# Moving the second layer's weight conversion and the experts' result stores in a retention + MoE + SoLU kernel

## Chip, core and metric

One core of a Trainium2 chip runs the whole kernel. The metric is the device time of one execution in microseconds (us). Time before: median 525.42 us of three runs (524.66 to 526.79).

Engines are named as in the profile: PE (TensorE, matmuls), PEld (its weight loads), DVE (VectorE), ACT (ScalarE), POOL (GpSimd), and SP, which here only issues DMAs. Each engine works through its instructions in program order, and an instruction that waits holds up everything behind it on its engine. "SPq" in a row is a DMA that SP issues.

## What is computed

Three stages follow each other: a retention over 768 steps (chunked into tiles), a top-2-of-8 mixture of experts, and a two-layer block with a SoLU between its layers.

```python
def _moe_ref(x, w_gate, w_noise, noise, w1, w2):      # x: 1536 x 512, 8 experts
    ...
    for e in range(E):
        for k in range(2):
            mask = top2[:, k] == e
            h = np.maximum(x[mask] @ w1[e], 0.0)       # 512 -> 1024
            out[mask] += top2_w[mask, k, None] * (h @ w2[e])   # 1024 -> 512

def _moe2_ref(x, w_in, w_out, g_ln):
    h = x @ w_in                                       # 512 -> 1024
    ...                                                # softmax of h, h * softmax, layer norm, g_ln
    return (ln @ w_out).astype(np.float32)             # 1024 -> 512
```

[...]

## The kernel before

**Matmuls in three terms.** Every fp32 operand is split into a high part (rounded to fp32r, by ACT) and a low part (the rest, by DVE): `xh`/`xl` for rows, `wh`/`wl` for weights, `hh`/`hl` for hidden values. A product is three matmuls: high x high, high x low, low x high.

**Experts.** A loop (lines 1051 to 1105) runs experts e = 0 to 6, sorted by load, with 448 down to 388 rows; the last one, e = 7 with 384 rows, has a code of its own (lines 1110 to 1154). The first layer (`hidden`) makes eight blocks f = 0..7 of 128 hidden columns: 12 matmuls into one PSUM bank, then ACT writes `hh` (line 707) and DVE writes `hl` (line 708). The banks alternate between the tags `b` and `a`, two of each, so block f can start only when `hl` of block f-4 is done. The second layer of e = 0..6 (`second`, line 1039) accumulates transposed results in the four banks c0..c3; during the first layer of the expert after it, `y_t` (line 1022) transposes each bank on DVE into `yr`, and after the fourth four DMAs on SP (line 1026) store it to `yg` in DRAM. The second layer of e = 7 (line 1146) makes rows at once: three row blocks b = 0, 1, 2, evicted by ACT (`y_rows`, line 1127) and stored to `yg`.

**Weights.** Weights arrive in units of 512 KB, eight for each expert and eight (64 to 71) for `w_in` (64 to 67) and `w_out` (68 to 71). `load_unit` issues the DMA on SP into one of four raw buffers `wr`; `split_unit` makes `wh` on ACT (line 194, for `w_out` line 190) and `wl` on DVE (line 195, for `w_out` line 191). `feed(split_to, load_to)` does both up to given units, and `advance(e, j)` calls it after each quarter of a layer.

**Conversion.** `convert_steps` is a generator of 16 jobs, eight for each of the two matrices, and `convert()` takes it one step further. A job has two steps: A (lines 117 to 119 on DVE, then line 120 on ACT) and B (lines 123 and 124 on DVE, which need ACT's result, then a DMA store on SP, line 125, and the load of a later job's raw bits, line 102). A first call only loads. So the generator is through after 33 calls. Before, e = 0 makes 6 calls and each of e = 1..6 makes 5 (two within the first layer, one after each of the last three quarters of the second); line 1108 would run the rest, and nothing is left by then.

**The way into the last block.** `weights` (line 668, called in the last expert after block 5) computes on DVE where each token's two results lie in `yg`. After block b = 0 of the last expert is stored, POOL gathers the results of the first tokens (line 799), ACT and DVE mix them (lines 809 and 810), and PE transposes the mixed rows (`x2_t`, line 819). That first transpose stands six hidden blocks into row block b = 2.

Of the kernel before, what the change touches and what calls it, by code (L numbers as in the profile page):

```python
# [44 lines left out]
def retnet_moe_solu(ctx, tc, qT, kT, k, v, w_gate, w_noise, noise, w1, w2, w_in, w_out, g_ln,  # L45
                    decay, out, dbg=None):
    nc = tc.nc
    B, NC, _, H, D = v.shape
# [3 lines left out]
    E = w1.shape[0]  # L52
# [28 lines left out]
    conv_jobs = []  # L81
    conv_ctx = ExitStack()
    def to_f32(w, name):
        if w.dtype == F32:
            return w
        rows, cols = w.shape
        f = dram.tile([rows, cols], F32, name=name)
        n = rows * cols // 128
        for c in range(0, n, 512):
            conv_jobs.append((w, f, c))  # L90
        return f

    def convert_steps():
        V = nc.vector
        cv = conv_ctx.enter_context(tc.tile_pool(name="cv", bufs=1, side="right", reuse_waits="tile"))
        view = lambda x, c: x.rearrange("(p r) f -> p (r f)", p=128)[:, c:c + 512]

        def load(n):
            if n < len(conv_jobs):
                w, _, c = conv_jobs[n]  # L100
                t = cv.tile([128, 512], I64, tag="raw", name="raw", bufs=2)
                nc.sync.dma_start(t, view(w, c))
                raws.append(t)

        raws = []
        load(0)
        for n, (w, f, c) in enumerate(conv_jobs):
            load(n + 1)
            yield
            raw = raws.pop(0)  # L110
            bits = raw.bitcast(I32).rearrange("p (n t) -> p n t", t=2)
            l, h = raw.bitcast(U32).rearrange("p (n t) -> p n t", t=2)[:, :, 0], bits[:, :, 1]
            m, e = (cv.tile([128, 512], I32, tag=t, name=t) for t in ("cm", "ce"))
            t = m.bitcast(F32)
            o = cv.tile([128, 512], F32, tag="co", name="co", bufs=2)

            V.tensor_scalar(m, h, 0xFFFFF, 1 << 20, op0=OP.bitwise_and, op1=OP.bitwise_or)
            V.scalar_tensor_tensor(t, l, 2.0 ** -32, m, op0=OP.mult, op1=OP.add)
            V.tensor_scalar(e, h, 0x7FF00000, None, op0=OP.bitwise_and)  # L119
            nc.scalar.activation(e, e, AF.Relu, bias=rebias, scale=8.0)  # L120
            yield

            V.scalar_tensor_tensor(e, h, -2 ** 31, e, op0=OP.bitwise_and, op1=OP.bitwise_or)
            V.scalar_tensor_tensor(o, t, 2.0 ** -20, e.bitcast(F32), op0=OP.mult, op1=OP.mult)
            nc.sync.dma_start(view(f, c), o)
# [3 lines left out]
    def convert():  # L129
        next(conv, None)  # L130
# [884 lines left out]
    def y_t(e, d):  # L1015

        if d == 0:
            yr_t[e] = ep.tile([128, CAP // 32, KD, 32], F32, tag="yr", name="yr")  # L1020
        n = SETS[e]
        nc.vector.transpose(yr_t[e][:, :n, d], PY[e][d][:, :32 * n])
        if d == KD - 1:
            dst = yg[OFF[e]:OFF[e + 1], :].rearrange("(b i) (a c) -> a i b c", i=32, a=4)
            for a in range(4):
                nc.sync.dma_start(dst[a], yr_t[e][32 * a:32 * a + 32, :n].rearrange("p b d j -> p b (d j)"))
            yr_t.pop(e)
            PY.pop(e)

    def second(e, j, py):  # L1030

# [12 lines left out]

    def advance(e, j):
        up = 8 * e + (AHEAD[j] if e or j > 3 else 5 + j)
        for n in range((0, 0, 0, 0, 2, 2, 1, 1)[j] if not e else j > 4):
            convert()
        feed(up, up + 3)

    for e in range(E - 1):
        if e:
            hidden_of(e)
        for j in range(4):
            for f in (2 * j, 2 * j + 1):
# [23 lines left out]
                    next(fresh, None)  # L1079
                if e and f in (1, 3, 4, 5):  # L1080
                    d = (1, 3, 4, 5).index(f)
                    y_t(e - 1, d)
                    y_bank(e, d)
                elif e and f in (2, 6):
                    convert()
                elif not e and f > 5:
                    for d in ((0, 1), (2, 3))[f - 6]:
                        y_bank(e, d)
            advance(e, j)
        for j in range(4):  # L1090
            unit_t.pop(8 * e + j)
        xgT.pop(e)
        py = PY[e]
        for j in range(4):
            second(e, j, py)
            for d in ((0, 1), (2, 3), (), ())[j] if e else ((), (0, 1), (2, 3), ())[j]:
                xg_t(e + 1, d)
            advance(e, 4 + j)
            if not e:
                fresh = fresh if j else load_xg(2)  # L1100
                for n in range(2 if j < 2 else 1):
                    next(fresh)
                rows = fresh
            elif j in (1, 2):
                next(fresh, None)


    for _ in conv:
        pass
    e = E - 1  # L1110
    hidden_of(e)
    for j in range(4):
        for f in (2 * j, 2 * j + 1):
            hidden(e, f, slice(0, CAPS[e]))
            if 0 < f <= KD:
                y_t(e - 1, f - 1)
            if f == 5:
                weights()
        advance(e, j)
    for j in range(4):  # L1120
        unit_t.pop(8 * e + j)
# [7 lines left out]
        nc.sync.dma_start(yg[OFF[-2] + b * 128:OFF[-2] + (b + 1) * 128], y)  # L1129

    w2_of = [unit_t.pop(8 * e + 4 + j) for j in range(4)]
    conv_ctx.close()
    gx_ctx.close()
    m2_ctx = ExitStack()
# [206 lines left out]
```

## Time and profile before

| | before |
|---|---|
| median of three runs | 525.42 us (524.66 to 526.79) |
| the profiled execution, its own time | 527.31 us |
| span of the profile, first to last instruction | 525.3 us |
| mean granted TensorE clock | 0.991 of full |
| PE busy | 508.4 us (97%) |
| DVE busy | 369.2 us (70%) |
| ACT busy | 231.3 us (44%) |
| POOL busy | 100.8 us (19%) |
| the 16 DMA engines, mean rate | 213 GB/s |

The page has the busy time of each engine, the span in 40 slices, the chain of work that ended last, and the costliest groups of instructions. The trace behind it gives the instructions in order of time, the waits by their releaser, and busy times of any stretch. Times within the span count from its first instruction. A busy PE is not a PE at its peak, since ends of pipelined matmuls are modelled; gaps between matmuls and the granted clock are to be read beside it.

### The profile page before, as it was taken

The page shows a single profiled execution, that of the slowest core. Times are in us where ns is not written, and L with a number is a line of the kernel's source. Part 1 is how long each engine was busy: PE and PEld are TensorE (multiplying, and loading weights), DVE is VectorE, ACT ScalarE, POOL GpSimd, SP SyncE. Part 2 cuts the span into 40 slices and gives each one's busy share as a digit, 9 for nine tenths or more (in the row PEclk, how much of TensorE's full clock was granted, in tenths as well). Part 3 has the DMA queues.
Part 4 walks back from the last instruction along what each step waited for, and adds up shares of the span by engine and source line. Part 5 has one row for each costly group of instructions (what it writes and reads, how often), then busy time and mean ns, then how long its engine had stood idle before and what let it go on. Part 6 is the DMA issues. An engine that isn't in the chain of part 4 may idle for free.

```text
span 525.3 us, 8618 instructions
## 1 busy us (share of the span) xinstructions
PE 508.4 (97%) x3059; PEld 464.2 (88%) x3059; DVE 369.2 (70%) x743; ACT 231.3 (44%) x434; POOL 100.8 (19%) x202
## 2 busy tenths in 40 slices
PE   8999999999999999999997999999799999999996
PEld 7888888999999999999997999998687788888886
DVE  5679888668668778878578778778167677656650
ACT  3487733435234334344235344445254535354441
POOL 4000001520404103004004000000444435511120
PEclk9999999999999999999998999999899999999999
DMA  8999432597898997969969985766471655553341
GB/s 251 321 401 326 157 112 61 183 353 232 277 313 193 358 299 154 356 203 234 360 194 267 304 217 192 224 162 166 140 220 43 207 164 160 162 188 101 100 121 46
DMA packets 71857, 111.92 MB, mean 213 GB/s; under 512 B 9760, under 2 KB 37152, under 8 KB 71808
## 3 DMA queue, kind: packets, MB, share of 16 engines
q1 hardware_dynamic: 65520, 94.58, 60.1%
q0 software_dynamic: 4944, 16.39, 9.8%
q8 instruction: 26, 0.43, 0.3%
q10 hardware_dynamic: 1344, 0.34, 0.3%
q14 instruction: 23, 0.19, 0.1%
HBM read 83.50 MB, written 27.79 MB: 212 GB/s over the span
## 4 chain that ended last, share of the span: by engine, by line
PE 57%; DVE 18%; DMA 12%; issue 5%; ACT 4%; SPq 2%; DVEq 0%; ACTq 0%
PE c L1039 14%; PE b L925 12%; PE d L838 9%; PE b L703 7%; PE a L703 7%; DMA wr<-in_moe_w_dram 4%; DVE wl L195 4%; DMA yg<-yr 2%; DMA xr<-xd,rows_r 2%; PE c L443 1%; PE s L426 1%; ACT wh L194 1%; DVE xt L1002 1%; DVE hl L708 1%; PE c L454 1%
## 5 line engine op out<-in xcount | busy, mean ns | idle before, releaser
L195 DVE TENSOR_TENSOR wl<-wr,wh 128x1024 fp32r<-128x1024 f32 x68 | 81.8, 1220 | 30.0 <-ACT wh L194 25.9
L194 ACT ACTIVATE wh<-wr 128x1024 fp32r<-128x1024 f32 x68 | 70.1, 1051 | 31.4 <-DMA wr<-in_moe_w_dram 31.2
L1039 PE MATMUL c<-hh,wh 128*128 128x448 f32 (+5 forms) x224 | 79.2, 354 | 0.3 <-DVE c L1013 0.3
L1039 PE MATMUL c<-hl,wh 128*128 128x448 f32 (+5 forms) x224 | 78.9, 352 | 0.0
L1039 PE MATMUL c<-hh,wl 128*128 128x448 f32 (+5 forms) x224 | 78.6, 351 | 0.0
L703 PE MATMUL b<-xh,wh 128*128 128x192 f32 (+8 forms) x144 | 47.5, 338 | 3.4 <-DVE hl L708 2.7
L703 PE MATMUL b<-xh,wl 128*128 128x192 f32 (+8 forms) x144 | 47.1, 335 | 0.0
L1039 PEld LDWEIGHTS c<-hh,wh 128*128 128x128 f32 x224 | 42.1, 188 | 1.9 <-issue 0.8
L799 POOL DMA_INDIRECT y<-yg,slot_y x24 | 24.9, 1036 | 96.2 <-DMA yg<-y 90.4
L703 PE MATMUL a<-xh,wl 128*128 128x256 f32 (+7 forms) x128 | 43.3, 342 | 0.0
L703 PE MATMUL a<-xh,wh 128*128 128x256 f32 (+7 forms) x128 | 43.3, 342 | 0.0
L1039 PEld LDWEIGHTS c<-hh,wl 128*128 128x128 f32 x224 | 42.2, 188 | 1.1
L1039 PEld LDWEIGHTS c<-hl,wh 128*128 128x128 f32 x224 | 42.1, 188 | 1.1
L925 PE MATMUL b<-wh,zh 128*128 128x512 f32 (+1 forms) x104 | 38.4, 376 | 0.5 <-ACT zh L914 0.5
L838 PE MATMUL d<-wh,x2h 128*128 128x512 f32 x96 | 38.8, 405 | 0.0
L925 PE MATMUL b<-wl,zh 128*128 128x512 f32 (+1 forms) x104 | 38.3, 375 | 0.0
L838 PE MATMUL d<-wl,x2h 128*128 128x512 f32 x96 | 38.0, 396 | 0.0
L838 PE MATMUL d<-wh,x2l 128*128 128x512 f32 x96 | 37.8, 394 | 0.0
L120 ACT ACTIVATE ce<-ce,rebias 128x512 int32<-128x512 int32 x16 | 11.6, 724 | 54.3 <-DVE ce L119 51.6
L1004 ACT ACTIVATE xh<-xt 128x428 fp32r<-128x428 f32 (+5 forms) x24 | 13.0, 540 | 51.1 <-DVE xt L1002 51.1
L1076 POOL COPY pace<-hh 1x1 f32<-1x1 f32 x20 | 8.2, 411 | 135.7 <-ACT hh L707 135.6
L968 POOL DMA_INDIRECT xr<-xd,rows_r x27 | 31.3, 1159 | 15.2 <-DMA xs<-xr 5.2
(244 smaller groups left out, 1081.1 us busy)
## 6 DMA issues: line engine op xcount, KB each, us to landing
wr<-in_moe_w_dram SPq DMA_DIRECT2D x60, 512.0 KB
zd<-zs SPq DMA_DIRECT2D x40, 128.0 KB
zc<-zd SPq DMA_DIRECT2D x10, 512.0 KB
xs<-xr SPq DMA_DIRECT2D x18, 256.0 KB
raw<-in_moe_w_in_dram SPq DMA_DIRECT2D x8, 512.0 KB
raw<-in_moe_w_out_dram SPq DMA_DIRECT2D x8, 512.0 KB
xq<-xs SPq DMA_DIRECT2D x16, 208.0 KB
yg<-yr SPq DMA_DIRECT2D x16, 208.0 KB
```

The lines of the kernel that those rows point to most:

```text
L120: nc.scalar.activation(e, e, AF.Relu, bias=rebias, scale=8.0)
L194: nc.scalar.activation(hi, t, AF.Copy)
L195: low = lambda: nc.vector.tensor_sub(lo, t, hi)
L426: nc.tensor.matmul(p[:, s, hp, :], KT[i][r, hp, :], QT[i][r, hp, :], start=True, stop=True)
L703: nc.tensor.matmul(p, w[:, 0, f * 128:(f + 1) * 128], x[:, d, c], start=(n == 0), stop=(n == len(terms) - 1))
L799: nc.gpsimd.indirect_dma_start(out=t, out_offset=None, in_=yg[:upto], in_offset=bass.IndirectOffsetOnAxis(ap=slot_y[:, i, s:s + 1], axis=0))
L838: nc.tensor.matmul(PH[i][:, s, :], x[:, c], w[:, 0, f], start=(n == 0), stop=(n == 3 * KD - 1))
L925: nc.tensor.matmul(p, z[:, f * 128:(f + 1) * 128], unit_t[8 * E + 4 + f // 2][n][:, f % 2, c], start=(m == 0), stop=(m == len(terms) - 1))
L968: nc.gpsimd.indirect_dma_start(out=t[b], out_offset=None, in_=xd[:], in_offset=bass.IndirectOffsetOnAxis(ap=rows_r[:, e - 1, b:b + 1], axi ...
L1004: nc.scalar.activation(hi, t, AF.Copy)
L1039: nc.tensor.matmul(py[d][:, :CAPS[e]], c, h[:, f, :CAPS[e]], start=(f == 0 and n == 0), stop=(f == KF - 1 and n == 2))
L1076: nc.gpsimd.tensor_copy(pace, H_t[e][0][:1, f, :1])
```

## The change

Four things are changed; the arithmetic stays as it is.

1. **When `convert()` is called.** e = 0 makes 3 calls in place of 6, each of e = 1..6 makes 4 in place of 5 (the call after the last quarter of the second layer is gone), and e = 7 gets a call after each of its eight blocks f. That is 3 + 24 = 27 calls by the end of e = 6, and the last six of the 33 (three A, three B) fall behind blocks 0 to 5 of e = 7. Line 1108's loop moves behind the first layer of e = 7, where nothing is left to run.
2. **What a job of `w_out` covers:** 128 whole rows in place of a strip of all rows, so that a unit of `w_out` rests on two jobs and not on all eight.
3. **Result stores of e = 0..5.** `y_t` becomes a generator. The four stores are no longer issued in a row after the fourth transpose: one follows `advance(e, 2)`, one the call behind block 6, one `advance(e, 3)`, and one the first `advance` of the second layer, each behind the weight loads which that `advance` issues.
4. e = 6's stores (during e = 7) stay four in a row.

```diff
         for c in range(0, n, 512):
-            conv_jobs.append((w, f, c))
+            if cols == 512:
+                view = lambda x, c: x[c // 4:c // 4 + 128, :]
+            else:
+                view = lambda x, c: x.rearrange("(p r) f -> p (r f)", p=128)[:, c:c + 512]
+            conv_jobs.append((w, f, c, view))
...
         if d == KD - 1:
             dst = yg[OFF[e]:OFF[e + 1], :].rearrange("(b i) (a c) -> a i b c", i=32, a=4)
+            y = yr_t.pop(e)
+            PY.pop(e)
             for a in range(4):
-                nc.sync.dma_start(dst[a], yr_t[e][32 * a:32 * a + 32, :n].rearrange("p b d j -> p b (d j)"))
-            yr_t.pop(e)
-            PY.pop(e)
+                if e < E - 2:
+                    yield
+                nc.sync.dma_start(dst[a], y[32 * a:32 * a + 32, :n].rearrange("p b d j -> p b (d j)"))
...
     def advance(e, j):
         up = 8 * e + (AHEAD[j] if e or j > 3 else 5 + j)
-        for n in range((0, 0, 0, 0, 2, 2, 1, 1)[j] if not e else j > 4):
+        if j in (5, 6) or not e and j == 7:
             convert()
         feed(up, up + 3)
...
                     d = (1, 3, 4, 5).index(f)
-                    y_t(e - 1, d)
+                    y_st = y_t(e - 1, d)
+                    next(y_st, None)
                     y_bank(e, d)
                 elif e and f in (2, 6):
                     convert()
+                    if f == 6:
+                        next(y_st, None)
...
             advance(e, j)
+            if e and j > 1:
+                next(y_st, None)
...
             advance(e, 4 + j)
+            if e and j == 0:
+                next(y_st, None)
...
-    for _ in conv:
-        pass
     e = E - 1
     hidden_of(e)
     for j in range(4):
         for f in (2 * j, 2 * j + 1):
             hidden(e, f, slice(0, CAPS[e]))
             if 0 < f <= KD:
-                y_t(e - 1, f - 1)
+                for _ in y_t(e - 1, f - 1):
+                    pass
             if f == 5:
                 weights()
+            convert()
         advance(e, j)
...
     w2_of = [unit_t.pop(8 * e + 4 + j) for j in range(4)]
+    for _ in conv:
+        pass
```

How the instructions stand now. The numbers behind names only tell instances of a tile apart, and lines after the change are 3 to 14 higher than before.

**DVE, from the second layer of e = 4 into the first of e = 5, before:**

```order
L195 TENSOR_TENSOR wl_3276<-wr_3194,wh_3275 128x1024
L117 TENSOR_SCALAR cm_3317<-raw_3133 128x512
L118 SCALAR_TENSOR_TENSOR cm_3317<-raw_3133,cm_3317 128x512
L119 TENSOR_SCALAR ce_3318<-raw_3133 128x512
L708 SCALAR_TENSOR_TENSOR hl_3325<-b_3326,hh_3324 128x396
L708 SCALAR_TENSOR_TENSOR hl_3325<-a_3346,hh_3324 128x396
```

The same place now:

```order
L126 SCALAR_TENSOR_TENSOR ce_3195<-raw_2880,ce_3195 128x512
L127 SCALAR_TENSOR_TENSOR co_3196<-cm_3194,ce_3195 128x512
L198 TENSOR_TENSOR wl_3240<-wr_3157,wh_3239 128x1024
L711 SCALAR_TENSOR_TENSOR hl_3282<-b_3283,hh_3281 128x396
L711 SCALAR_TENSOR_TENSOR hl_3282<-a_3303,hh_3281 128x396
```

The step A that stood between the last `wl` of the second layer and `hl` of block 0 is gone.

**DVE, blocks 0 to 3 of the last expert, before** (`c0`, `c1` are e = 6's result banks):

```order
L708 SCALAR_TENSOR_TENSOR hl_3996<-b_3997,hh_3995 128x384
L708 SCALAR_TENSOR_TENSOR hl_3996<-a_4012,hh_3995 128x384
L1022 STREAM_TRANSPOSE yr_4027<-c0_3715 128x13x32
L195 TENSOR_TENSOR wl_4030<-wr_3898,wh_4029 128x1024
L195 TENSOR_TENSOR wl_4034<-wr_3936,wh_4033 128x1024
L708 SCALAR_TENSOR_TENSOR hl_3996<-b_4047,hh_3995 128x384
```

The same now, from the last quarters of e = 6's second layer on:

```order
L198 TENSOR_TENSOR wl_3931<-wr_3851,wh_3930 128x1024
L711 SCALAR_TENSOR_TENSOR hl_3964<-b_3965,hh_3963 128x384
L120 TENSOR_SCALAR cm_3980<-raw_3790 128x512
L121 SCALAR_TENSOR_TENSOR cm_3980<-raw_3790,cm_3980 128x512
L122 TENSOR_SCALAR ce_3981<-raw_3790 128x512
L711 SCALAR_TENSOR_TENSOR hl_3964<-a_3987,hh_3963 128x384
L1025 STREAM_TRANSPOSE yr_4002<-c0_3669 128x13x32
L126 SCALAR_TENSOR_TENSOR ce_3981<-raw_3790,ce_3981 128x512
L127 SCALAR_TENSOR_TENSOR co_3982<-cm_3980,ce_3981 128x512
L198 TENSOR_TENSOR wl_4010<-wr_3853,wh_4009 128x1024
L198 TENSOR_TENSOR wl_4014<-wr_3899,wh_4013 128x1024
L711 SCALAR_TENSOR_TENSOR hl_3964<-b_4027,hh_3963 128x384
```

A step A now stands ahead of `hl` of blocks 1, 3 and 5, and a step B behind the transposes that follow blocks 1 and 3; the last B stands behind `weights`, ahead of unit 65's `wl` and `hl` of block 6. On ACT the line-120 instruction of each A stands ahead of `hh` of blocks 1, 3 and 5. Ahead of what is shown, the last quarters of e = 6's second layer now hold an A before unit 60's `wl` and a B before unit 61's.

**SP, the queue ahead of the first loads of `w_out`, before:**

```order
L174 DMA wr_4083<-w_in32_70 32x1024 x4
L1026 DMA yg_68<-yr_4027 32x13x128 x4
L176 DMA wr_4146<-w_out32_71 128x2x512
L176 DMA wr_4194<-w_out32_71 128x2x512
L1129 DMA yg_68<-y_4230 128x512
```

The same place now:

```order
L177 DMA wr_4073<-w_in32_70 32x1024 x4
L1033 DMA yg_68<-yr_4002 32x13x128 x4
L128 DMA w_out32_71<-co_4100 128x512
L179 DMA wr_4146<-w_out32_71 128x2x512
L179 DMA wr_4194<-w_out32_71 128x2x512
L1141 DMA yg_68<-y_4230 128x512
```

The store of the last conversion job, which waits for that job's step B on DVE, now stands ahead of the loads of units 68 and 69 and of the first row store of the last expert.

## Rows read from the trace of the kernel before

**Rows 1.** Page, part 1: busy us, share of the span, instructions.

```profile
PE 508.4 (97%) x3059; PEld 464.2 (88%) x3059; DVE 369.2 (70%) x743; ACT 231.3 (44%) x434; POOL 100.8 (19%) x202
```

**Rows 2.** Waits of PE by line and releaser: us in total, times, longest.

```profile
PE b L703 <- DVE hl L708: 2.7, 1, 2.7
PE a L819 <- DVE t L810: 2.7, 1, 2.7
```

**Rows 3.** Busy time of stretches: us; PE, PEld, DVE, ACT, POOL; PEclk; DMA share; GB/s.

```profile
280.60:284.00 3.40, 3.40 (x13) 3.39 (x12) 3.32 (x6) 1.69 (x4) 3.23 (x4) 0.52 1.19 187
...
341.80:358.50 16.70, 16.70 (x98) 16.70 (x97) 11.97 (x27) 7.26 (x12) 0.00 (x0) 1.00 0.70 169
```

**Rows 4.** Order of time, PE and DVE, start of e = 5: start, us, instruction [idle before].

```profile
279.66 0.45 PE L703 MATMUL b<-xh,wh 128*128 128x396 f32 x1 [2.73 <-DVE hl L708]
...
272.77 1.22 DVE L195 TENSOR_TENSOR wl<-wr,wh 128x1024 fp32r<-128x1024 f32 x1 [1.74 <-ACT wh L194]
273.92 0.69 DVE L123 SCALAR_TENSOR_TENSOR ce<-raw,ce 128x512 int32<-128x512 int32 x1
...
275.24 1.22 DVE L195 TENSOR_TENSOR wl<-wr,wh 128x1024 fp32r<-128x1024 f32 x1
276.38 0.42 DVE L117 TENSOR_SCALAR cm<-raw 128x512 int32<-128x512 int32 x1
...
277.44 0.42 DVE L119 TENSOR_SCALAR ce<-raw 128x512 int32<-128x512 int32 x1
279.04 0.57 DVE L708 SCALAR_TENSOR_TENSOR hl<-b,hh 128x396 fp32r<-128x396 f32 x1 [1.17 <-ACT hh L707]
```

**Rows 5.** Order of time, ACT, start of e = 5.

```profile
277.90 0.72 ACT L120 ACTIVATE ce<-ce,rebias 128x512 int32<-128x512 int32 x1 [4.21 <-DVE ce L119]
278.52 0.48 ACT L707 ACTIVATE hh<-b 128x396 fp32r<-128x396 f32 x1
```

**Rows 6.** Order of time, DVE, first layer of the last expert.

```profile
340.51 2.36 DVE L195 TENSOR_TENSOR wl<-wr,wh 128x1024 fp32r<-128x1024 f32 x2 [0.39 <-ACT wh L194]
344.58 0.56 DVE L708 SCALAR_TENSOR_TENSOR hl<-b,hh 128x384 fp32r<-128x384 f32 x1 [1.71 <-ACT hh L707]
346.61 0.56 DVE L708 SCALAR_TENSOR_TENSOR hl<-a,hh 128x384 fp32r<-128x384 f32 x1 [1.46 <-ACT hh L707]
347.08 0.61 DVE L1022 STREAM_TRANSPOSE yr<-c 128x416 f32<-128x416 f32 x1
347.61 2.32 DVE L195 TENSOR_TENSOR wl<-wr,wh 128x1024 fp32r<-128x1024 f32 x2
349.85 0.55 DVE L708 SCALAR_TENSOR_TENSOR hl<-b,hh 128x384 fp32r<-128x384 f32 x1
...
354.93 0.56 DVE L708 SCALAR_TENSOR_TENSOR hl<-a,hh 128x384 fp32r<-128x384 f32 x1 [0.94 <-ACT hh L707]
...
359.34 1.23 DVE L195 TENSOR_TENSOR wl<-wr,wh 128x1024 fp32r<-128x1024 f32 x1
360.48 0.55 DVE L708 SCALAR_TENSOR_TENSOR hl<-b,hh 128x384 fp32r<-128x384 f32 x1
```

**Rows 7.** Order of time, SP, ACT, POOL, DVE and PE, last expert's end.

```profile
356.93 4.04 SPq L176 DMA_DIRECT2D wr<-w_out  x2
...
362.11 1.34 ACT L190 ACTIVATE wh<-wr,gcol 128x512 fp32r<-128x512 f32 x2 [1.16 <-DMA wr<-w_out]
364.29 1.34 ACT L190 ACTIVATE wh<-wr,gcol 128x512 fp32r<-128x512 f32 x2 [0.84 <-DMA wr<-w_out]
365.53 0.58 ACT L1127 ACTIVATE y<-c 128x512 f32<-128x512 f32 x1
...
369.13 0.97 POOL L799 DMA_INDIRECT y<-yg,slot_y  x1 [83.22 <-DMA yg<-y]
...
375.45 0.75 DVE L810 SCALAR_TENSOR_TENSOR t<-y,top_w,t 128x512 f32<-128x512 f32 x1 [8.99 <-DMA y<-yg,slot_y]
...
376.26 1.11 PE L819 MATMUL a<-unit,t 128*128 128x128 f32 x4 [2.73 <-DVE t L810]
```

More of the change, by code (lines that the diff above doesn't have):

```diff
@@ L95, in convert_steps @@
         cv = conv_ctx.enter_context(tc.tile_pool(name="cv", bufs=1, side="right", reuse_waits="tile"))
-        view = lambda x, c: x.rearrange("(p r) f -> p (r f)", p=128)[:, c:c + 512]
         def load(n):
             if n < len(conv_jobs):
-                w, _, c = conv_jobs[n]
+                w, _, c, view = conv_jobs[n]
                 t = cv.tile([128, 512], I64, tag="raw", name="raw", bufs=2)
@@ L106, in convert_steps @@
         load(0)
-        for n, (w, f, c) in enumerate(conv_jobs):
+        for n, (w, f, c, view) in enumerate(conv_jobs):
             load(n + 1)
```

## Prediction, made before the changed kernel ran

> **What bounds the kernel now.** First the page's busy shares: PE works 508.4 us of a span of 525.3, DVE has 30% to spare [rows 1]. PE works through its matmuls nearly without a gap, so an edit on DVE, ACT or SP counts only where PE comes to wait for it. Second, therefore, PE's list of waits: from the first expert to the last block it has two waits that matter, 2.7 us each [rows 2]. Third, the order of time around each.
>
> The first wait lies in e = 5. Block 4 of the first layer starts at 279.66 after 2.73 us of idleness [rows 4]; it needs the bank of block 0, free when `hl` of block 0 is written. DVE starts that `hl` at 279.04. Ahead of it stands a step A (276.38 to 277.86), and behind A a wait of 1.17 us: A's ACT instruction (277.90) stands ahead of `hh` (278.52) in ACT's queue [rows 4, 5]. After the gap the granted clock is 0.52 of full from 280.60 to 284.00 [rows 3], between the levels 1.2 and 2.4 GHz, so this stretch does 3.40 x 0.52 = 1.77 us of full-clock work and loses 1.63 us. The wait costs 2.73 + 1.63 = 4.36 us.
>
> The second wait is the way into the last block. PE takes the first mixed rows at 376.26 after 2.73 us idle [rows 7]. Going back: mixed at 375.45, gathered from 369.13, after the row store of block b = 0, which ACT evicts at 365.53. ACT is late there: it first splits units 68 and 69, whose DMAs it awaits (1.16 and 0.84 us idle) [rows 7]. Unit 69's load needs the raw buffer of unit 65, free when DVE ends that unit's `wl` (359.34 + 1.23 = 360.57) [rows 6]; the load is there at 364.29, 3.72 us later. So whatever delays this `wl` delays the eviction, the gather and PE, microsecond for microsecond: nothing behind the gather is slack, as PE already waits.
>
> **Step one: the wait in e = 5.** The A ahead of `hl` of block 0 is removed, with its ACT instruction. With all else as it was, `hl` starts at 276.38, where A started, and ends at 276.94; PE was ready at 279.66 - 2.73 = 276.93. The wait goes, and its slow clock. What is late next: behind block 2 of e = 5 now stands an A (before, a B). From 276.38: two `hl` (0.48 each), a transpose with its clearing (0.6), two `wl` (2.24, from 347.61 to 349.85 in [rows 6]), `hl` of block 2 (0.48), A (1.48), its wait (1.17): `hl` of block 3 starts at 283.3 and ends at 283.9. Block 7 could start at 276.93 + 3 x 2.16 = 283.4, taking 2.16 us for a block, a little over the last expert's 16.70 / 8 = 2.09 [rows 3]. So 0.5 us returns. Gain: 4.36 - 0.5 = 3.9 us; bounds 4.4 and 0 (a late weight or row DMA could keep DVE just as late).
>
> **Step two: the last expert.** Costs of a conversion on DVE: A takes 1.48 us (276.38 to 277.86), B 1.32 (273.92 to 275.24), and an A ahead of an `hl` also 1.17 of waiting, ahead of a `wl` 1.74 [rows 4]. A `wl` takes 1.14 (275.24 to 276.38), an `hl` 0.47, a transpose 0.53 [rows 4, 6]. Before, DVE is free at 340.51 - 0.39 = 340.12 and by 344.58 is waiting for PE [rows 6], so the start is level with PE. Now, in DVE's order:
> - A 1.45, wait 1.74, `wl` 60 1.14, B 1.32, `wl` 61 1.14: `hl` of block 0 at 346.9 (before 344.58).
> - `hl` 0.47, A 1.48, wait 1.17: block 1 at 350.0 (346.61).
> - `hl` 0.47, transpose 0.53, B 1.32, two `wl` 2.24: block 2 at 354.6 (349.85).
> - `hl`, transpose, A, wait, 3.65: block 3 at 358.2.
> - `hl`, transpose, B, `wl` 64, 3.46: block 4 at 361.7.
> - 3.65 again: block 5 at 365.35 (354.93).
> - `hl` and `weights`, 4.41 (354.93 to 359.34), then the last B 1.32: `wl` 65 from 371.1 to 372.3 (359.34 to 360.57), and `hl` of block 6 at 372.2 (360.48).
>
> That is 11.7 us late, all on DVE and ACT in turn. PE feels it first by its banks (blocks 6 and 7 wait for `hl` of 2 and 3, about 2 us in all), then in row block b = 0, whose matmuls take the hidden blocks in order and stand before `hl` of 5 and 6: PE finishes b = 0 at about 374, some 10 us later than before.
>
> The chain to the mix is later still. Unit 69's load lands at 372.3 + 3.72 = 376.0. Unit 68's load no longer rests on the last conversion's data (the finer jobs see to that), but it stands behind that job's store in SP's queue, as the SP rows of the change show, and the store waits for B: it issues at about 371.1 + 0.4 = 371.5. Its landing is bounded by 3.7 us (as unit 69's) and by 5.2 us (356.93 to 362.11 in [rows 7], which holds other transfers): 375.2 to 376.7. Two splits of 1.24 to 1.34 us follow on ACT [rows 7], so the eviction of b = 0 comes at 377.8 to 379.3 in place of 365.53: 12.2 to 13.8 us late. I take 13.0, the middle, since now only one store lies ahead of the load. From there the chain is as before (10.7 us to PE), so PE takes the mixed rows at 389.2. In between PE has b = 1 and most of b = 2, and waits for the rest; a slow clock on the way is paid out of that wait, and the one behind it is paid before the change as well.
>
> **Step three: the rest.** The stores of e = 0..5 move past weight loads on SP. They are the same bytes, PE nowhere waits for a weight or a store in its list of waits, and `yr` is wanted again only an expert later: 0 us, with a cover of several us. If that cover were gone, DVE would come late by one store. The calls dropped in e = 0..6 empty DVE and ACT where PE, but for e = 5, waits for neither: 0 us. Since they may bring DVE earlier into e = 6's second layer, or later DMAs hold it longer, I allow the start of step two 2 us either way. The new strips of `w_out` change no byte count: 0 us.
>
> **Sum.** +13.0 - 3.9 = +9.1 us. The profiled execution took 527.31 us for a span of 525.3, 1.9 over the median; the sum is made in its span and added to the median: 525.4 + 9.1 = 534.5 us. Its own range: down by 2.0 (DVE early), 0.8 (unit 68 early) and 0.5 (more gain), to 531.2; up by 2.0, 0.8 and about 1 of the gain, to 538.3.
>
> **Rivals.**
> *The room on DVE covers it.* In the last expert's first layer DVE is busy 11.97 of 16.70 us [rows 3], so 4.7 us are free. Three A and three B are 8.4 us. If the idle moments took the work and no ACT round trip were added, the lateness would be 8.4 - 4.7 = 3.7 us, and 3.7 - 3.9 is no change: 525.2 us. Against it: the row of the 1.17 us wait shows that A and `hl` do not overlap, and `weights` and five `wl` leave no place to catch up. For it: PE's banks let `hl` be four blocks late. The Trainium skill speaks for this reading: its page "Perfetto Trace Analysis", section "Identifying the Most-Contended Engine", calls occupancy a fair measure of how close VectorE and ScalarE are to their limit. By occupancy alone the sum would be this rival's; the trace's rows of waits speak against using it for one stage of two engines in turn.
>
> *The wait in e = 5 stays* (a late weight DMA keeps DVE late there, as SP's queue is reordered): no gain, and the whole loss, 525.4 + 13.0 = 538.4 us.
>
> *Faster: the last expert absorbs the steps.* If DVE entered e = 7 so early, and the round trips hid so well, that `wl` 65 still ended by 360.6, nothing would be late behind it, and only the gain stayed: 525.4 - 3.9 = 521.5 us. It turns to a loss from the point where that `wl` ends more than 3.9 us late. All 8.4 us would have to fit into 4.7, with the A and B ahead of block 0 hidden too; before, DVE already waits for PE at block 0 and so cannot start early.
>
> That the conversion isn't in fact moved is excluded by the order of the changed program.
>
> **Chances.** Forecast 0.71, stays-and-loses 0.12, covered 0.10, faster 0.07. A measurement of this kernel tells about 0.5%, 2.6 us, from no change. Forecast and second rival are slower by more: 0.83; covered is the same: 0.10; faster 0.07. Forecast and second rival together hold over 8 in 10, and their bounds make the range: from 530.5 (a little under the forecast's own low end) to 538.8.
>
> **What would show it.** In the changed profile: no PE wait of 2.7 us for `hl` near 277, and a clock of 1.0 there; in the last expert `hl` of blocks 1, 3 and 5 each 1.2 us behind an A, `hl` of block 6 some 12 us behind its place; PE waits for `hl` in row block b = 0 of 6 us or more; ACT waiting for `w_out` until 375 or later; the first gather some 13 us later against PE's start of e = 7. All these times move forward by the gain in e = 5. It is wrong if DVE is level with PE at block 5 of e = 7, or if the gather's start moves by less than 6 us, or if PE gets a new wait in e = 1..6.

## The result, and the profile after

The changed kernel takes 531.51 us (median of 22 runs, 528.96 to 533.78), the kernel before on the same chip 526.75 us (22 runs, 521.82 to 531.17): a ratio of 1.0103, with a 95% interval of 1.0085 to 1.0122. It is slower by 4.8 us, where the prediction said 9.1; the time lies in the predicted range (530.5 to 538.8), near its low end. Some of that is luck: the range was built on a median of 525.42 for the kernel before, which took 1.3 us more in this comparison, and 4.8 us on top of 525.42 would have been 530.2, just below the range.

The profiled execution has a span of 531.1 us, 5.8 more than before. Four marks on PE divide the span: the first matmul of e = 1, the first of the last expert, the first transpose of the mixed rows (`x2_t`), and the end.

| us | until e = 1 | e = 1 to 6 | last expert to `x2_t` | from there to the end |
|---|---|---|---|---|
| before | 120.18 | 221.52 | 34.56 | 149.0 |
| after | 121.50 | 216.70 | 45.28 | 147.6 |
| difference | +1.3 | -4.8 | +10.7 | -1.4 |
| predicted | 0 | -3.9 | +13.0 | 0 |

Read first the busy shares (page, part 1 [rows 1]) and PE's list of waits [rows 2], here from 120 to 400 us:

```profile
PE 509.5 (96%) x3059; PEld 463.1 (87%) x3059; DVE 368.7 (69%) x743; ACT 231.4 (44%) x434; POOL 98.3 (19%) x202
```

```profile
PE c L1160 <- DVE hl L711: 4.3, 1, 4.3
PE a L822 <- DVE t L813: 2.6, 1, 2.6
PE c L1160 <- ACT hh L710: 1.8, 2, 1.2
PE a L706 <- DVE hl L711: 1.3, 1, 1.3
```

The work is the same. The wait of 2.7 us in e = 5 has gone; the one for the mixed rows is still there, and three lines are new, all in the last expert (L1160 is its second layer, L706 the first). The order of time on DVE at the start of e = 5 [rows 4] shows why the first has gone. PE's first matmul of e = 5 is at 268.57:

```profile
272.42 1.23 DVE L198 TENSOR_TENSOR wl<-wr,wh 128x1024 fp32r<-128x1024 f32 x1 [1.74 <-ACT wh L197]
273.56 0.68 DVE L126 SCALAR_TENSOR_TENSOR ce<-raw,ce 128x512 int32<-128x512 int32 x1
...
274.89 1.22 DVE L198 TENSOR_TENSOR wl<-wr,wh 128x1024 fp32r<-128x1024 f32 x1
276.03 0.56 DVE L711 SCALAR_TENSOR_TENSOR hl<-b,hh 128x396 fp32r<-128x396 f32 x1
```

`hl` of block 0 follows the weights at once, 7.5 us after PE's first matmul; before it was 11.6. Before, an A of 1.48 us and a wait of 1.17 stood between. The first layer of the last expert has them now, on DVE [rows 6]; PE's first matmul there is at 338.20:

```profile
342.91 0.55 DVE L711 SCALAR_TENSOR_TENSOR hl<-b,hh 128x384 fp32r<-128x384 f32 x1
...
346.03 0.56 DVE L711 SCALAR_TENSOR_TENSOR hl<-a,hh 128x384 fp32r<-128x384 f32 x1 [1.17 <-ACT hh L710]
...
350.60 0.55 DVE L711 SCALAR_TENSOR_TENSOR hl<-b,hh 128x384 fp32r<-128x384 f32 x1
...
354.21 0.56 DVE L711 SCALAR_TENSOR_TENSOR hl<-a,hh 128x384 fp32r<-128x384 f32 x1 [1.17 <-ACT hh L710]
...
361.25 0.56 DVE L711 SCALAR_TENSOR_TENSOR hl<-a,hh 128x384 fp32r<-128x384 f32 x1 [1.17 <-ACT hh L710]
...
365.53 0.68 DVE L126 SCALAR_TENSOR_TENSOR ce<-raw,ce 128x512 int32<-128x512 int32 x1
...
366.86 1.22 DVE L198 TENSOR_TENSOR wl<-wr,wh 128x1024 fp32r<-128x1024 f32 x1
367.99 0.55 DVE L711 SCALAR_TENSOR_TENSOR hl<-b,hh 128x384 fp32r<-128x384 f32 x1
```

`wl` of unit 65 starts 28.7 us after PE's first matmul of this expert; before it was 359.34 - 341.70 = 17.6 [rows 6]. The 11 us go on through SP, ACT, POOL and PE to the mixed rows [rows 7]:

```profile
366.97 0.34 SPq L128 DMA_DIRECT2D w_out<-co  x1
367.40 1.07 SPq L179 DMA_DIRECT2D wr<-w_out  x2
...
371.34 2.81 ACT L193 ACTIVATE wh<-wr,gcol 128x512 fp32r<-128x512 f32 x4 [5.55 <-DMA wr<-w_out]
374.05 0.58 ACT L1139 ACTIVATE y<-c 128x512 f32<-128x512 f32 x1
376.84 0.60 ACT L1139 ACTIVATE y<-c 128x512 f32<-128x512 f32 x1 [2.21 <-PE c L1160]
...
377.67 0.97 POOL L802 DMA_INDIRECT y<-yg,slot_y  x1 [94.27 <-DMA yg<-y]
...
383.48 0.66 PE L822 MATMUL a<-unit,t 128*128 128x128 f32 x4 [2.60 <-DVE t L813]
```

### The profile page after: what moved, and what is told of

It reads as the page before. It is cut to its first block, busy times and chain, and to the rows that moved or that the text cites. A ratio compares the mean times of both kernels' runs of the same rounds, so it can differ in the third digit from the quotient of the medians.

```text
span 531.1 us, 8610 instructions
## 1 busy us (share of the span) xinstructions
PE 509.5 (96%) x3059; PEld 463.1 (87%) x3059; DVE 368.7 (69%) x743; ACT 231.4 (44%) x434; POOL 98.3 (19%) x202
## 4 chain that ended last, share of the span: by engine, by line
PE 49%; DVE 18%; DMA 15%; issue 9%; ACT 5%; SPq 1%; POOL 0%; POOLq 0%; DVEq 0%; ACTq 0%
PE b L928 11%; PE c L1044 11%; PE d L841 9%; DMA wr<-in_moe_w_dram 8%; PE b L706 5%; PE a L706 4%; DVE wl L198 3%; DVE xt L1005 2%; ACT wh L197 2%; DVE hl L711 2%; DMA wr<-w_in 2%; PE s L429 2%; PE c L446 1%; DMA qt<-in_qT_dram 1%; ACT xh L1007 1%
## 5 line engine op out<-in xcount | busy, mean ns | idle before, releaser
L706 PE MATMUL b<-xh,wh 128*128 128x192 f32 (+8 forms) x144 | 47.3, 336 | 0.6 <-DVE hl L711 0.3
L706 PE MATMUL b<-xh,wl 128*128 128x192 f32 (+8 forms) x144 | 46.6, 332 | 0.0
L706 PE MATMUL a<-xh,wh 128*128 128x256 f32 (+7 forms) x128 | 43.2, 341 | 1.3 <-DVE hl L711 1.3
L706 PE MATMUL a<-xh,wl 128*128 128x256 f32 (+7 forms) x128 | 42.8, 339 | 0.0
L123 ACT ACTIVATE ce<-ce,rebias 128x512 int32<-128x512 int32 x16 | 11.6, 723 | 54.1 <-DVE ce L122 48.9
L854 ACT ACTIVATE ee<-d,st 128x1024 f32<-128x1024 f32 x12 | 13.4, 1116 | 42.1 <-DVE st L847 39.0
```

The costliest lines, as they stand in the source:

```text
L706: nc.tensor.matmul(p, w[:, 0, f * 128:(f + 1) * 128], x[:, d, c], start=(n == 0), stop=(n == len(terms) - 1))
L854: nc.scalar.activation(ee, ph, AF.Exp, bias=col(0), accum_out=col(1))
```

## The experiments

Three questions: what ended the wait in e = 5, what the last expert's 10.7 us are made of, and which of the change's parts is worth keeping. All ratios are to the kernel before in the same comparison. The marks of each run's profiled execution:

| run | ratio (95% interval) | until e = 1 | e = 1 to 6 | last expert to `x2_t` | to the end |
|---|---|---|---|---|---|
| e1 stores moved, blocks | 0.9920 (0.9888 to 0.9952) | 119.65 | 216.66 | 34.85 | 147.4 |
| e12 the same again | 0.9955 (0.9923 to 0.9987) | 120.62 | 216.63 | 34.34 | 149.1 |
| e8 stores in a row behind the loads, blocks | 0.9966 (0.9932 to 1.0001) | 120.60 | 217.28 | 34.79 | 148.9 |
| e9 stores moved, strips | 0.9989 (0.9966 to 1.0013) | 120.53 | 220.22 | 34.44 | 149.3 |
| e11 blocks alone | 0.9948 (0.9915 to 0.9982) | 120.61 | 219.97 | 34.73 | 149.1 |
| e2 the change, stores as before | 1.0102 (1.0061 to 1.0143) | 121.22 | 215.55 | 45.03 | 149.0 |
| e10 the change again | 1.0099 (1.0056 to 1.0141) | 121.25 | 215.55 | 43.81 | 147.4 |
| e6 the change with strips | 1.0159 (1.0106 to 1.0212) | 121.28 | 215.55 | 45.27 | 149.2 |
| e5 the change, no ACT step in the last jobs | 1.0045 (1.0012 to 1.0079) | 120.77 | 215.54 | 40.04 | 149.1 |
| e7 the change, last store behind a load | 1.0125 (1.0065 to 1.0185) | 120.70 | 216.82 | 45.37 | 147.7 |
| e4 the change, four steps in the last expert | 1.0038 (1.0004 to 1.0072) | 121.49 | 216.82 | 39.21 | 149.1 |
| e3 the change, none there | 0.9988 (0.9959 to 1.0017) | 119.75 | 219.79 | 34.87 | 150.4 |

**Stores or conversion calls (e1, e2).** e1 takes the conversion calls back and keeps the rest; e2 takes the stores back:

```diff
# e1
-        if j in (5, 6) or not e and j == 7:
+        for n in range((0, 0, 0, 0, 2, 2, 1, 1)[j] if not e else j > 4):
             convert()
...
-            convert()
# e2
             for a in range(4):
-                if e < E - 2:
-                    yield
```

> The change's store order and w_out jobs, but conversion calls as before (6 in e = 0, 5 in each of e = 1..6, none in e = 7). Theory 'conversion': the stores move nothing that PE waits for. PE's wait of 2.7 us at block 4 of e = 5 stays, the wait at the mixed rows stays 2.7 us, and the time is that of before: ratio 1.000, within 0.995 to 1.005. Rival 'stores': taking the store bursts out of the weight loads' way is what freed e = 5; then the wait of 2.7 us is gone here, and the ratio is 0.990 to 0.993.

> The change's conversion calls and w_out jobs, with the four result stores in a row as before. Theory 'conversion': the whole of the changed time is here: ratio 1.010, within 1.006 to 1.015; no wait of 2.7 us in e = 5; unit 65's low part on DVE starts 28 us after the last expert's first matmul, as with the whole change. Rival 'stores': the wait in e = 5 is still there, and the ratio is 1.016 to 1.020.

In both the wait of e = 5 is gone, and e = 1 to 6 takes 217 and 215.5 us. So the two gains do not add: there is one wait of some 4 us, and either edit removes it. e2 has the whole loss of the last expert. We read e1 at first as a gain of the stores. That was too quick: both runs hold the blocks of `w_out` too, which we had taken for nothing. (That the moved calls need no blocks for it, e6 below shows: it has strips, and 215.55 us. No run has the calls alone.)

**Stores or blocks (e8, e9, e11, e12).** e8 is e1 with the four stores in a row at the first one's new place; e9 is e1 with strips; e11 is the kernel before with the blocks and nothing else. Strip and block each cover 128 of the 1024 rows of `w_out`, which arrive as 64-bit floats (4 KB a row) and are stored as 32-bit floats (2 KB a row): a strip is every eighth row (not columns, as the expectation of e6 has it), a block 128 rows in succession.

```diff
# e8
-            if e and j > 1:
-                next(y_st, None)
+            if e and j == 2:
+                for _ in y_st:
+                    pass
# what e9 takes out of e1, e6 out of the change, and e11 adds to before
             if cols == 512:
                 view = lambda x, c: x[c // 4:c // 4 + 128, :]
```

> The first run's kernel (stores moved, conversion calls as before; ratio 0.992) with the four stores of an expert's results in a row again, but at the place where the first of them now stands, behind the loads of advance(e, 2), and not at their old place ahead of those loads. Theory “behind the loads”: the gain of 4 us is that the weights' load no longer stands behind 4.3 us of stores on SP (in before the load of 255.80 leaves behind the stores of 251.22); a burst behind it brings the same: ratio 0.990 to 0.994, no wait of over 1 us at the start of e=5. Theory “one by one”: the burst now stands ahead of the xs stores and the loads of the next blocks and holds those up instead: ratio 0.996 to 1.001, and a wait of over 1.5 us of TensorE for hl or xs comes back.

> The kernel before with the moved stores and nothing else: the conversion calls and the strips of the second layer's jobs are as before (the first run had the blocks of 128 rows beside the moved stores). Theory “order of stores and loads on SP”: the same as the first run, ratio 0.990 to 0.995, 216 to 218 us from the first matmul of e=1 to that of the last expert. Theory “blocks help”: part of the gain was that of the blocks' smoother writes; ratio 0.996 to 1.000 and a wait of over 1 us of TensorE in e=1 to e=6.

> The kernel before with one edit: the second layer's conversion jobs read and write blocks of 128 rows (the four stores in a row at their old place, the conversion calls as before). What is known: stores moved and blocks together 0.992, stores moved with strips 0.9989, so the blocks have a part in it. Theory “blocks alone”: while the DMA engines are full in e=4 (8 to 12 us behind its first matmul) the jobs with strips move 190 GB/s and those with blocks 245, and this alone frees the weights' loads; ratio 0.990 to 0.995, no wait of over 1 us of TensorE from e=1 to e=6. Theory “both are needed”: the four stores at their old place still hold the load behind them, ratio 0.996 to 1.000 and a wait of 1 to 2.5 us in e=5.

> The first run's kernel again (stores moved, blocks, conversion calls as before), beside the kernel with the blocks alone: ratio 0.989 to 0.996, no wait of over 1 us of TensorE from e=1 to e=6, 216 to 217.5 us from the first matmul of e=1 to that of the last expert. If its 0.992 was scatter, 0.997 or more and a wait in e=5.

With strips the moved stores bring nothing that can be measured; the wait in e = 5 is back. PE's waits of e9:

```profile
PE a L819 <- DVE t L810: 2.6, 1, 2.6
PE b L703 <- DVE hl L708: 2.4, 1, 2.4
```

With blocks alone the median is 0.5% faster, as good as with blocks and moved stores in the same comparison (523.56 and 523.86 us). What the blocks do shows in e = 4, ahead of that wait, in the 10 us that begin 7.5 to 8 us after its first matmul. The rows give PE, PEld, DVE, ACT, POOL, the clock, the share of the DMA engines and GB/s, for before, e9, e1 and e11:

```profile
240.00:250.00 10.00, 10.00 (x56) 10.00 (x55) 8.24 (x15) 4.43 (x7) 3.45 (x5) 1.00 1.10 240
```

```profile
240.00:250.00 10.00, 10.00 (x56) 10.00 (x55) 8.58 (x17) 4.32 (x7) 3.69 (x5) 1.00 1.09 262
```

```profile
239.40:249.40 10.00, 10.00 (x56) 10.00 (x56) 8.64 (x15) 2.86 (x5) 2.83 (x3) 1.00 1.07 340
```

```profile
243.60:253.60 10.00, 10.00 (x56) 10.00 (x55) 8.57 (x17) 2.86 (x5) 3.79 (x5) 1.00 1.07 338
```

The DMA engines are full in all four, but with strips (the first two) they have moved 240 to 262 GB/s and with blocks 338 to 340. The windows do not hold quite the same transfers, since slow ones push later ones out; in the first 4 us alone it is 187 and 195 GB/s with strips and 243 to 256 in the four runs with blocks and the calls as before (e1, e8, e11, e12). (A share can pass 1, since a packet counts whole where it starts.)

From there it is a straight way to the wait. Behind the raw load of that stretch SP issues three loads of weights, and ACT comes to wait for the first of them. Rows of SP and ACT, before and e11 (their first matmuls of e = 4 are at 232.11 and 235.65), with DVE's `hl` of block 0 of e = 5 in e11:

```profile
240.89 3.43 SPq L176 DMA_DIRECT2D wr<-in_moe_w_dram  x3
...
254.20 1.06 ACT L194 ACTIVATE wh<-wr 128x1024 fp32r<-128x1024 f32 x1 [5.63 <-DMA wr<-in_moe_w_dram]
```

```profile
243.81 3.25 SPq L179 DMA_DIRECT2D wr<-in_moe_w_dram  x3
...
254.26 1.06 ACT L197 ACTIVATE wh<-wr 128x1024 fp32r<-128x1024 f32 x1 [2.79 <-DMA wr<-in_moe_w_dram]
...
279.08 0.57 DVE L711 SCALAR_TENSOR_TENSOR hl<-b,hh 128x396 fp32r<-128x396 f32 x1 [1.18 <-ACT hh L710]
```

With strips ACT has these weights 13.3 us (before) and 12.8 (e9) after the issue, with blocks 10.5 (e11) and 11.1 (e1). DVE's `wl` follows ACT, and DVE carries the lateness into e = 5: there `hl` of block 0 starts 11.6 us [rows 4] and 10.6 after PE's first matmul with strips, 8.2 and 8.1 with blocks. The A and its wait of 1.18 us still stand ahead of this `hl` in e11 and e1, and cost PE nothing there: it took the late weights and the A together to make the wait.

Two things stay open. The profiled execution of e11 is the slowest of its twelve (526.66 us) and has a wait of its own, 2.2 us for `hl` in e = 3. Whether the moved stores add to the blocks is therefore not settled: e = 1 to 6 takes 216.6 us with them and 220 without, but most of that is this one wait (e = 5 alone takes 34.6 to 34.7 and 34.9), and the medians see no difference. And e8, the stores in a row behind the loads, lies between (0.9966), with a wait of 0.6 us in e = 5.

**What the last expert pays for (e3, e4, e5).** e3 moves its six calls to e = 0; e4 keeps those after blocks 0 to 3 and moves two; e5 leaves out ACT's instruction of the last three jobs:

```diff
# e3
-        if j in (5, 6) or not e and j == 7:
+        for n in range((0, 0, 0, 0, 2, 2, 2, 3)[j] if not e else j in (5, 6)):
             convert()
# e4
+        for n in range((0, 0, 0, 0, 1, 2, 1, 1)[j] if not e else j in (5, 6)):
...
-            convert()
+            if f < 4:
+                convert()
# e5
-            nc.scalar.activation(e, e, AF.Relu, bias=rebias, scale=8.0)
+            if n < 13:
+                nc.scalar.activation(e, e, AF.Relu, bias=rebias, scale=8.0)
```

> The whole change, but the six steps of e = 7 are called in the second layer of e = 0 (9 calls there in place of 3). Theory 'conversion': the gain of e = 5 without the last expert's loss: no wait in e = 5, unit 65's low part back at 17 to 18 us after the last expert's first matmul, PE's wait at the mixed rows 2.7 us again; ratio 0.990 to 0.994 (4 to 5 us faster than before). Rival 'the steps cost wherever they are': e = 0 and the start of e = 1 get waits on PE of 3 us or more, and the ratio is 0.997 or higher.

> The whole change, but only blocks 0 to 3 of e = 7 call a conversion step; the last A and the last B (behind block 4 and behind the index work) are called in e = 0. Theory 'serial': DVE is rid of A 1.48, its wait 1.17 and B 1.32, so unit 65's low part comes 4.0 us earlier (24.4 us after the last expert's first matmul instead of 28.4), and PE's mixed rows as much earlier: ratio 1.001 to 1.004. Rival 'room': only steps beyond DVE's idle time cost, all of the loss sits in the last two steps, and the ratio falls to 0.995 or lower.

> The changed kernel without ScalarE's middle instruction of the last three conversion jobs (those of the last expert; the last quarter of the second layer's converted weights is wrong by that). In the changed kernel the second VectorE step of such a job waits for ScalarE, and three evictions of the last expert (at 346.03, 354.21 and 361.25) stand 1.17 us behind their predecessor for ScalarE's hh. Theory “round trips”: the three conversion steps wait on VectorE for ScalarE, and ScalarE's hh queues behind them; without the instruction the conversion costs VectorE its two operations alone, about 0.6 us each. The last expert, from its first matmul to x2_t, goes from 45.3 us to 41.5 to 43, the ratio to before from 1.010 to 1.003 to 1.006. Theory “VectorE's work alone”: the queue is longer by the operations themselves and the waits only fill in; 44.5 to 45.5 us, ratio 1.008 to 1.012.

e3 has the last expert back at 34.87 us, so the steps cause all of the 10.7. It is no faster than before, since the nine calls in e = 0 make a new wait in e = 1 and e = 1 to 6 takes 219.8. Its row of PE:

```profile
131.82 0.47 PE L706 MATMUL b<-xh,wh 128*128 128x448 f32 x1 [2.18 <-DVE hl L711]
```

e4 takes a third of the steps away. DVE enters the expert as in e10 (the change again), its first `wl` 0.5 us ahead of PE's first matmul, and the expert is 4.6 us faster (39.21 against 43.81), about half of the loss. `wl` of unit 65 comes 3.9 us earlier (23.2 us after the first matmul against 27.1), as theory 'serial' has it (4.0); of the rest, 0.5 us lies between there and the eviction of b = 0, where unit 68's load no longer stands behind the store of a late B. e5 keeps all DVE work and takes only ACT out of it. `wl` of unit 65 starts 23.3 us after the first matmul (336.31), in the change again (e10, 336.80) 27.1. Their rows of DVE:

```profile
359.60 1.22 DVE L199 TENSOR_TENSOR wl<-wr,wh 128x1024 fp32r<-128x1024 f32 x1
```

```profile
363.86 1.22 DVE L198 TENSOR_TENSOR wl<-wr,wh 128x1024 fp32r<-128x1024 f32 x1
```

These 3.8 us are the three waits of 1.17 us and 0.3 more, and they arrive at `x2_t` whole (40.04 against 43.81). So of the 9.4 us that DVE is late in e10 (27.1 - 17.6), two fifths are the way through ACT, the rest DVE's own work.

**Strips, and the last store (e6, e7, e10).** e6 is the change with strips; e7 issues the last job's store behind the load of unit 68; e10 is the change itself:

```diff
# e7
+            if n == len(conv_jobs) - 1:
+                yield
             nc.sync.dma_start(view(f, c), o)
...
+    feed(n_units - 2, n_units - 2)
     for _ in conv:
         pass
```

> The whole change, but the second layer's jobs write strips (four columns of every row group) as before, not blocks of 128 rows. Then the load of the first block of those weights (unit 68) depends on every job, the last one too, as it does in the changed kernel on one only. Theory “landing”: the loads of units 68 and 69 stand behind the landing of the last store; in the changed kernel 68 leaves 0.43 us behind the store at 366.97 and its first user waits until 371.34; with strips both leave some 2 us later: the way from the first matmul of the last expert to x2_t becomes 47 to 48 us, ratio 1.013 to 1.016. Theory “block or strip is nothing”: that wait is hidden in the queue; 44.5 to 46 us, ratio 1.008 to 1.012.

> The whole change, but the sixth conversion call of the last expert is left to its end, and the last store is issued behind the load of the first block of the second layer's weights (unit 68), which does not read it. Theory “VectorE”: what holds the last expert is VectorE's queue, which is 11 us late at wl65 in the changed kernel; the load that leaves earlier brings 0 to 1.5 us: 44 to 45.5 us from the first matmul of the last expert to x2_t, ratio 1.007 to 1.011. Theory “queue of SP”: ScalarE waited 5.55 us for that load at 371.34, the longest wait of the chain; the load issued up to 4 us earlier brings all of it: 41 to 42.5 us, ratio 1.002 to 1.005.

> The changed kernel again, as the measure of how far the stages of one and the same program move between two profiled executions. Expected: ratio 1.008 to 1.013; 216 to 218 us from the first matmul of e=1 to that of the last expert and 44.8 to 45.6 from there to x2_t. If the 1.3 us by which it came late to e=1 belongs to the change, that first matmul is at 121.2 or later again; if it is scatter, between 120 and 121.

e6 and e10 are a close pair: both enter the last expert after 215.55 us, with DVE 0.5 us ahead of PE. Rows of SP and ACT, e6 and then e10:

```profile
363.99 0.34 SPq L125 DMA_DIRECT2D w_out<-co  x1
366.06 0.90 SPq L176 DMA_DIRECT2D wr<-w_out  x2
...
370.12 2.65 ACT L190 ACTIVATE wh<-wr,gcol 128x512 fp32r<-128x512 f32 x4 [7.32 <-DMA wr<-w_out]
```

```profile
363.96 0.34 SPq L128 DMA_DIRECT2D w_out<-co  x1
364.40 1.07 SPq L179 DMA_DIRECT2D wr<-w_out  x2
...
368.41 2.75 ACT L193 ACTIVATE wh<-wr,gcol 128x512 fp32r<-128x512 f32 x4 [5.63 <-DMA wr<-w_out]
```

With strips the load depends on the last store too and leaves 2.07 us behind it in place of 0.44, and all that follows is later: the eviction of b = 0 by 1.6 us, `x2_t` by 1.46. So the blocks earn some 1.6 us at this place as well. (e6 misses the 47 to 48 us of 'landing', though its ratio of 1.0159 lies there; e10 misses both of its stretches, 216 to 218 and 44.8 to 45.6.)

How much of such a gain reaches `x2_t` depends on one thing more. e2 has blocks and DVE's lead of 0.5 us too, and evicts b = 0 where e10 does (34.25 and 34.27 us after the first matmul), yet it reaches `x2_t` 1.2 us later (45.03). In the 6 us behind PE's long wait in b = 0, from 365.80 to 371.80, the granted clock is 0.55 in e2 and 0.68 in e10, between the levels 1.2 and 2.4 GHz; b = 1 is evicted 0.7 us later, and its row store is issued 0.45 us ahead of the second gather in place of 1.2. Rows of SP, POOL (the second gather) and DVE (the mix that needs it), e2 and then e10:

```profile
375.46 0.33 SPq L1140 DMA_DIRECT2D yg<-y  x1
...
375.91 0.95 POOL L802 DMA_INDIRECT y<-yg,slot_y  x1 [0.30 <-issue]
...
380.99 0.75 DVE L813 SCALAR_TENSOR_TENSOR t<-y,top_w,t 128x512 f32<-128x512 f32 x1 [9.04 <-issue]
```

```profile
374.77 0.33 SPq L1141 DMA_DIRECT2D yg<-y  x1
...
375.96 0.95 POOL L802 DMA_INDIRECT y<-yg,slot_y  x1 [0.30 <-issue]
...
379.80 0.75 DVE L813 SCALAR_TENSOR_TENSOR t<-y,top_w,t 128x512 f32<-128x512 f32 x1 [7.81 <-ACT t L812]
```

All 14 traces fall into these two groups. Where the store is issued 0.2 to 0.5 us ahead of the second gather (before, e1, e2, e3, e7, e8, e9, e11, e12), the mix starts 4.8 to 5.4 us behind the gather, and `x2_t` 10.5 to 11.0 behind the eviction of b = 0. Where it is 0.9 us or more (the change, e4, e5, e6, e10), these are at most 3.6 to 3.9 (in four of the five the mix waits for ACT by then) and 9.3 to 9.6. No edit moved that store alone, and why it delays the gather is open.

So the load that leaves earlier still (e7: at 360.82, ahead of the store) brings nothing to the time. b = 0 is evicted 1.4 us earlier than in the first profile of the change (34.45 against 35.85), half of which is DVE's earlier start, but b = 1, which PE holds up by its wait for `hl`, is evicted where it was (38.41 and 38.64). Its store is then issued 0.3 us ahead of the second gather, and `x2_t` stays where it was.

The best version is e1 (and e12): 522.12 and 523.86 us, against 526.13 and 526.71 for the kernel before beside them.

## Why the prediction came out as it did

*Sign and mechanism: right.* DVE and ACT work in turn, the last expert's steps stand in DVE's order ahead of `hl`, and their lateness goes through to the mixed rows. The foretold signs are there: three `hl` 1.2 us behind an A, waits in row block b = 0 (4.3 us for `hl` and 1.8 for `hh`; foretold were 6 or more for `hl` alone), no wait near 277 and a clock of 1.00 there. `wl` 65 came 11.0 us late, foretold 11.7. The room on DVE did not cover it, and e3 shows that it is the steps and nothing else. The Trainium skill's rule on that rival ("Perfetto Trace Analysis", "Identifying the Most-Contended Engine": occupancy tells how near VectorE and ScalarE are to their limit) misleads for this one stage: DVE was busy 11.97 of 16.70 us [rows 3], and three jobs still made it 9.4 (e10) to 11.0 us late.

*Step two, the size: 13.0 foretold, 10.7 and (e10) 9.3 measured.* Two terms were off. The first is DVE's start. By the prediction's own steps DVE's first `wl` came 1.6 us behind PE's first matmul (340.12 + 1.45 + 1.74 - 341.70); it came 1.1 behind in the change and 0.5 ahead in e10. From that `wl` to the one of unit 65 it is 27.6 us in both, foretold 27.8: the chain of steps and waits was right, and what it missed is the start, by 0.5 and 2.1 us, for which the prediction allowed 2. So the eviction of b = 0 was 12.0 and 10.4 us late, foretold 12.2 to 13.8. The second term is the 10.7 us from there to PE, taken as fixed, which were 9.4 and 9.6: before, the row store of b = 1 is issued 0.3 us ahead of the second gather, in the change and e10 1.2 to 1.5, as shown above. The prediction had no term for that; e2 and e7, where it is 0.3 to 0.5 again, have the 10.7 back (10.8 and 10.9). A slow clock on the way there was foretold as paid out of PE's wait, and was: PE still waits 2.6 us at `x2_t`.

*Step one: 3.9 foretold, 4.8 and 6.0 measured.* The wait went as foretold; e2, e5, e6 and e10, with 215.5 us, show more than the upper bound of 4.4, which held the one wait and its slow clock alone. The rest lies in the same two experts: from before to e10, e = 5 goes from 39.8 to 34.6 us and e = 6 from 34.5 to 33.9, and with the long wait a wait of 0.4 us has gone from e = 5 and one of 0.3 from e = 6. The first profile of the change has two short waits in e = 5 (0.35 and 0.16 us), where it takes 35.7.

*Step three: the zero for the jobs of `w_out` failed.* The prediction held that their new form changes "no byte count: 0 us". The bytes are the same, but blocks alone make the kernel before 0.5% faster. (The 1.6 us that they are worth at the last load are another matter: step two had reckoned with them, since there unit 68's load no longer rests on the last job.) The zero for the moved stores stands by itself (e9: 0.9989), while with blocks they may add something. That the error did not show in the sum is luck: the conversion calls had already removed the wait that the blocks remove.

*The slow clock behind the mixed rows: foretold as paid "before as well".* It was not paid after. The stretch behind `x2_t`, before and after; the granted clock is the third number from the end:

```profile
376.20:382.00 5.80, 5.74 (x20) 4.77 (x21) 1.36 (x3) 1.80 (x3) 0.15 (x1) 0.71 0.38 123
```

```profile
383.40:389.00 5.60, 5.52 (x28) 4.62 (x29) 1.38 (x3) 2.01 (x4) 1.19 (x2) 1.00 0.77 227
```

PE idles about as long in both (2.73 and 2.60 us), yet only one has the fall. That is the -1.4 us of the last column. It is not the change's: the clock stays up in four of the 14 traces, the change, e10, e7 and e1, which has the calls as before, and falls in e2, e4, e5 and e6, which have calls in the last expert. In this profile the change had the luck of it.

*The start: +1.3, foretold 0.* The change, e2, e4, e6 and e10 reach e = 1 at 121.2 to 121.5, e5 and e7, which are the same up to there, at 120.7 to 120.8, and before at 120.18. Counted from its own first matmul, e = 0 takes 48.6 us in before and in e1, e3, e8, e9, e11 and e12, and 48.9 (e7) to 49.8 us in the change and the others, so about 1.0 of the 1.3 belongs to the change. About 0.7 us is a new wait for `xl` in the second layer of e = 0, which most of them have and e7 has not; why was not settled.

Summed: last expert -2.3 to -3.7, e = 1 to 6 -0.9 to -2.1, behind it -1.4 to -1.6, start +1.1 to +1.3 against the forecast. That makes 5.8 and 2.7 us in the two profiles; the medians say 4.8.

## What to carry to other kernels

Work that two engines do in turn costs its round trip at every step, and moving it into a stage whose evictions queue on the same two engines can cost more than the work itself, however idle they look on average (9.4 us of lateness for 8.4 us of DVE's work). Where two edits each remove the same wait, only one is paid for: measure them apart before giving up microseconds elsewhere for one of them. One profile of each kernel is not enough for terms of a microsecond: the clock behind `x2_t` and the place of one store moved stages by 1.2 to 1.5 us between traces of kernels that were alike up to there. And an edit that leaves the byte count alone still needs its own run: here the part that was costed at nothing was the one that paid by itself.

## What the runs showed of the hardware

- The same bytes in the same number of packets seem to cost the DMA engines different time by their place in DRAM, the one thing in which strips and blocks differ. Part 3 of the page (packets, MB, share of 16 engines' span), before and e11:

```profile
q1 hardware_dynamic: 65520, 94.58, 60.1%
```

```profile
q1 hardware_dynamic: 65520, 94.58, 59.4%
```

  That is 315.7 and 311.5 us of all engines. The Trainium skill ("DMA: Bandwidth & Descriptors", "Why small descriptors are slow (HBM only)") explains slow transfers by the size of the packets; packet counts and bytes are equal here, so that section does not tell the two apart. Over all runs the ranges touch (strips 313.5 to 315.7, blocks 308.8 to 313.7), so the stretch in e = 4 is the stronger sign, and what makes a strip slow is open.
- After waits of 1.9 to 4.3 us at one and the same place, `x2_t`, the granted clock fell in ten executions (0.71 over the stretch behind before's 2.73 us, 0.51 at first behind e8's 2.96) and stayed at 1.00 in four (behind the change's 2.60 and e1's 3.02), so the length of the idle time alone does not decide it.
